# Seven block products for three more batches, in a fused linear attention and mixer kernel

## The chip, the cores and the metric

The kernel runs on one core of one Trainium2 chip. The metric is the device time of one launch in microseconds (us). The kernel before takes 263.8 us, the median of three runs that lie between 263.64 and 263.93 us. One further run was recorded by the profiler, and its span of instructions is 262.1 us. All times "in the trace" are counted from the start of that span.

A core has engines that run their own instruction streams side by side: the tensor engine (PE in the profile, with PEld for its weight loads), the vector engine (DVE), the scalar engine (ACT), the general engine (POOL) and the engine that mostly issues transfers (SP). In the trace each engine runs its instructions in the order in which the program gives them.

## The reference

Eight batches of eight heads, 576 positions and a head width of 64 go through a linear attention, and its output, 576 x 512 for each batch, through a mixer: one two-layer network over the positions, one over the 512 channels with 1536 hidden channels.

```python
phi = lambda x: np.where(x > 0, x, np.exp(x) - 1.0) + 1.0
kv  = einsum('bhsd,bhse->bhde', phi(k), v);  z = phi(k).sum(axis=2)
x   = einsum('bhsd,bhde->bhse', phi(q), kv) / (einsum('bhsd,bhd->bhs', phi(q), z) + 1e-6)
h   = np.maximum(x.T @ w_tok1, 0.0) @ w_tok2       # over the positions, each batch
u   = x + h.T
h2  = np.maximum(u @ w_ch1, 0.0) @ w_ch2           # over the channels: 512 -> 1536 -> 512
out = u + h2
```

The last product, `relu(u @ w_ch1) @ w_ch2`, is the "second channel mixing" that the change is about. In the kernel its left factor is called `cr` (1536 hidden channels on 12 blocks of 128 partitions, 512 positions), and its right factor `wc2`. Of the 576 positions of a batch 512 are handled as four tiles of 128; the 64 that are left over of two neighbouring batches share one more tile, `crt`, called the pair's tail here.

## The kernel before

The program is a hand-made schedule. For each batch `n` from 2 on there is one stretch ("the stage of batch n") in which the tensor engine does the two channel mixings of batch `n`, and everything that batches `n+1` and `n+2` need is dropped in between at numbered places:

```python
    def run(bigs, fill):
        for i, big in enumerate(bigs):
            big()
            for s, fn in fill:          # all that stands at place i, after big number i
                if s == i:
                    fn()
```

The list of large pieces and their fillings, for batches 2 to 7 (before):

```python
    AT = {"kv": 0, "nd00": 2, "nd01": 3, "nd10": 4, "nd11": 5, "nd20": 6, "nd21": 7,
          "mm1": 9, "mm2a": 11, "mm2b": 12, "mm2t": 14, "uta": 11, "utb": 12, "utt": 14}
    for n in range(2, B):
        p, b = divmod(n, 2)
        if b == 0:
            big = m3(n) + (m4s(n) if n + 2 == B else m4(p, [0, 1, 2, 3]))
        else:
            big = m3(n) + m3t + m4(p, [4, 5, 6, 7, 8])
            if n + 1 == B:
                big = m3(n) + m3t + m4s(n) + [ ... mm4_last, in two column pieces ]
        fill = []
        if n + 1 < B:
            fill += [((AT3 if n == 2 else AT)[nm], fn) for nm, fn in steps(n + 1)]
        if n + 2 < B:
            d = 1 if n == 2 else 0
            fill += [(s + d, lambda g=g: phi("q", n + 2, g)) for g, s in ((0, 8), (1, 9))]
            fill += [(12 + d, lambda: qtr_dma(n + 2))]
            ...                                               # loads of batch 5, in stage 2
            fill += [(s + d, lambda g=g: prep_k(n + 2, g)) for g, s in ((0, 14), (1, 16))]
            fill += [(18, lambda: load_all(n + 4, "qkv"))]
        if n + 3 == B:
            fill += [(18 + i, lambda i=i: weight_sums(2 * i, 2)) for i in range(3)]
        if n + 2 >= B:
            fill += [(9, lambda n=n: row_sums(n, 3, 0, KH))]
            fill += [(s, lambda n=n, w=w, k0=k0: row_sums(n, w, k0, 3))
                     for s, k0 in ((10, 0), (12, 3)) for w in (1, 2, 4)]
        run(big, sorted(fill, key=lambda e: e[0]))
```

`m3` is the first channel mixing, 12 pieces of four matmuls of 512 columns; `m3t` is the same for the pair's tail, three pieces. `steps(n+1)` is the attention of the next batch: `kv`, six `nd` pieces (numerators and denominators), `mm1` and `mm2` (the mixing over positions, in two halves a and b, and `mm2t` for the tails of a pair), and the transposes `uta`, `utb`, `utt`, which are transfers. `phi("q", ..)` and `prep_k` prepare the batch after that: an exponential on ACT, then an addition `y` and a minimum (`qp` or `kp`) on DVE.

The second channel mixing is there in two forms. The plain form `m4` does one tile of 128 positions by 12 matmuls of 512 columns and one addition on DVE. The other form, `m4s`, is a scheme with seven block products in place of eight (both factors are cut into 2 x 2 blocks). It is used for batches 6 and 7 before the change:

```python
    def row_sums(n, which, k0, m):      # sums of blocks of cr, on DVE, written into sb[0..3]
        ks = slice(k0, k0 + m)
        a11, a12, a21, a22 = [ablock(n, i, e)[:, ks] for e in range(2) for i in range(2)]
        x_, y_, op = {1: (a21, a22, ALU.add), 2: (sb[0][:, ks], a11, ALU.subtract),
                      3: (a11, a21, ALU.subtract), 4: (a12, sb[1][:, ks], ALU.subtract)}[which]
        nc.vector.tensor_tensor(out=sb[which - 1][:, ks], in0=x_, in1=y_, op=op)

    def product(n, j, i):               # block product i for half j (256 positions)
        lhs, rhs, tile_, first = {
            1: (a_(0, 0), wblock(0, 0), "X", True), 2: (a_(1, 0), wblock(1, 0), "Z", True),
            6: (sb[1][:, :, j], tb[1], "X", False), 5: (sb[0][:, :, j], tb[0], "Y", True),
            7: (sb[2][:, :, j], tb[2], "X", False), 4: (a_(1, 1), tb[3], "X", False),
            3: (sb[3][:, :, j], wblock(1, 1), "Y", False)}[i]
        ...                             # "first" takes a new PSUM bank, the others add onto it
        for k_ in range(KH):            # 6 matmuls of 256 columns
            nc.tensor.matmul(out=ps, lhsT=lhs[:, k_], rhs=rhs[:, k_], start=(first and k_ == 0), ...)
        ...                             # after each of 1, 2, 6, 4, 3 one addition of 128 x 256 on DVE
                                        # from the bank (X, Z or Y) to o_sb; after 7 two (X and Y)
    ORDER = [(1, 0), (1, 1), (2, 0), (6, 0), (2, 1), (6, 1), (5, 0), (7, 0), (5, 1), (7, 1),
             (4, 0), (3, 0), (4, 1), (3, 1)]        # (product, half)
```

So the bank X of a half gets products 1, 6, 7 and 4 added up in it, and DVE reads it after each: product 6 may not start before DVE has read X after product 1, product 7 not before it was read after product 6, and so on. The block sums of the weights, `tb`, are made once by POOL (`weight_sums`, 18 instructions); `tb` and `sb` lie in input buffers whose data are used up.

The inputs of each batch are loaded by SP into `raw[name, n % 2]`, two buffers for each of q, k and v.

## Time and profile before

| what | value |
|---|---|
| time, median of three runs | 263.8 us |
| span of the profiled run | 262.1 us |
| mean granted clock of the tensor engine | 0.992 |
| stage of batch 3 in the trace | from 112.35 to 144.22 us |
| stage of batch 4 | from 144.22 to 171.47 us |
| stage of batch 5 | from 171.47 to 203.34 us |
| stage of batch 6 | from 203.34 to 230.36 us |
| stage of batch 7 and the end | from 230.36 to 262.1 us |

The stages are read from the chain of work that ended last, where each begins with the first piece of `m3`. Where the profile gives a group of instructions, its line has the busy time and the mean duration of one, then the idle time of the engine just before them and what ended that idle time. In a timeline each line is: start, duration, engine, line of the program, operation, output <- inputs with their shapes, the count, and in brackets how long the engine had been idle and what released it. Neighbouring instructions of an engine overlap a little, so the distance between two starts is the better measure of what one costs in a row.

### The profile page before, as it was taken

What the parts mean: (1) busy time and instruction counts of PE and PEld (TensorE: products, weight loads), DVE (VectorE), ACT (ScalarE), POOL (GpSimd) and SP (SyncE); (2) the same over time, 40 slices, a digit from 0 to 9 for tenths busy, and PEclk for the clock granted to TensorE, in tenths of its full rate; (3) what the DMA queues carried; (4) which work ended last, traced back from release to release, by engine and by line L of the source; (5) the groups of instructions that cost most, each with busy time, mean ns of one, the idle gap of its engine ahead of it and who ended that gap; (6) DMA issues with size and microseconds to landing.
All of it is one profiled execution on the core that took longest, in us unless ns stands there. A gap on an engine that the chain in (4) does not pass through costs nothing.

```text
span 262.1 us, 5249 instructions
## 1 busy us (share of the span) xinstructions
PE 249.9 (95%) x2142; PEld 138.4 (53%) x2142; DVE 161.9 (62%) x317; ACT 131.2 (50%) x205; POOL 65.6 (25%) x92
## 2 busy tenths in 40 slices
PE   7799999999999999999999999999999999999990
PEld 3574465646644544455644544455644545756970
DVE  5875859865966376837652575838862486815550
ACT  4755853387580569146670569046670543046100
POOL 9850300110011100110003100179909500060060
PEclk9999999999999999999999999999999999999996
DMA  7999999799049951899999972660083403350033
GB/s 254 254 204 293 351 232 399 243 265 407 9 114 198 393 210 25 179 258 406 409 253 172 373 277 42 149 164 0 16 156 81 123 0 23 80 160 3 0 100 103
DMA packets 49576, 48.35 MB, mean 184 GB/s; under 512 B 30288, under 2 KB 35536, under 8 KB 49552
## 3 DMA queue, kind: packets, MB, share of 16 engines
q1 hardware_dynamic: 41184, 34.35, 43.6%
q0 software_dynamic: 8208, 13.54, 23.3%
q8 instruction: 17, 0.28, 0.5%
q10 hardware_dynamic: 160, 0.13, 0.2%
q14 instruction: 7, 0.06, 0.1%
HBM read 35.85 MB, written 9.44 MB: 173 GB/s over the span
## 4 chain that ended last, share of the span: by engine, by line
PE 79%; DMA 10%; POOL 3%; DVE 2%; issue 1%; ACT 1%; POOLq 0%; DVEq 0%
PE c_ps L480 28%; PE h_ps L506 26%; DMA wc<-in_moe_w_ch_dram 7%; PE a_ps L246 6%; PE c_ps L494 4%; PE h_ps L259 4%; PE nd_ps L208 3%; PE h_ps L605 3%; DMA cr<-in_v_dram 3%; PE kv_ps L167 2%; PE y_ps L605 1%; POOL out_dram L629 1%; DVE o_sb L611 1%; POOL qT L673 1%; DVE ut L284 1%
## 5 line engine op out<-in xcount | busy, mean ns | idle before, releaser
L487 ACT ACTIVATE cr<-c_ps 128x512 bf16<-128x512 f32 x91 | 53.5, 599 | 77.2 <-PE c_ps L480 77.1
L480 PE MATMUL c_ps<-uT,wc 128*128 128x512 bf16 x384 | 91.4, 379 | 0.1
L506 PE MATMUL h_ps<-wc,cr 128*128 128x512 bf16 x288 | 66.0, 379 | 0.4 <-DMA wc<-in_moe_w_ch_dram 0.4
L480 PEld LDWEIGHTS <-wc 128*128 128x128 bf16 x384 | 35.7, 98 | 36.7 <-issue 1.7
L528 POOL DMA_DIRECT2D out_dram<-o_sb x24 | 14.5, 608 | 130.8 <-DVE o_sb L523 130.6
L506 PEld LDWEIGHTS <-cr 128*128 128x128 bf16 x288 | 27.4, 98 | 32.2 <-DMA wc<-in_moe_w_ch_dram 0.9
L220 DVE TENSOR_TENSOR x<-nd_ps,den 128x512 bf16<-128x512 f32 (+1 forms) x42 | 25.3, 602 | 1.5
L523 DVE TENSOR_TENSOR o_sb<-h_ps,u 128x512 f32<-128x512 f32 x24 | 16.4, 689 | 13.2 <-PE h_ps L506 13.0
L124 ACT ACTIVATE e<-q_raw 128x1152 bf16<-128x1152 f32 x16 | 18.5, 1160 | 5.6 <-DMA q_raw<-in_q_dram 5.4
L138 DVE TENSOR_TENSOR qp<-e,y 128x1152 bf16<-128x1152 bf16 x16 | 12.3, 770 | 12.3 <-ACT e L124 11.8
L124 ACT ACTIVATE e<-k_raw 128x1152 bf16<-128x1152 f32 x16 | 18.7, 1169 | 2.4 <-DMA k_raw<-in_k_dram 2.4
L217 DVE TENSOR_SCALAR den<-nd_ps 128x8 f32<-128x8 f32 (+1 forms) x42 | 6.9, 163 | 19.9 <-PE nd_ps L208 19.2
L271 DVE TENSOR_TENSOR u<-h_ps,x 128x1024 bf16<-128x1024 f32 x12 | 14.7, 1222 | 6.2 <-PE h_ps L259 6.2
L629 POOL DMA_DIRECT2D out_dram<-o_sb x16 | 8.3, 527 | 40.4 <-DVE o_sb L611 40.4
L138 DVE TENSOR_TENSOR kp<-e,y 128x1152 bf16<-128x1152 bf16 x16 | 12.1, 757 | 8.0 <-ACT e L124 7.4
L208 PEld LDWEIGHTS <-qT 128*128 128x128 bf16 x140 | 11.4, 98 | 9.3 <-issue 0.2
L208 PE MATMUL nd_ps<-kvbd,qT 128*128 128x130 bf16 x140 | 15.1, 223 | 0.0
L246 PE MATMUL a_ps<-x,w 128*128 128x512 bf16 x56 | 14.4, 379 | 0.0
L130 DVE TENSOR_SCALAR y<-q_raw 128x1152 bf16<-128x1152 f32 x16 | 13.6, 849 | 0.9 <-DMA q_raw<-in_q_dram 0.9
L149 ACT CAST vs<-v_raw 128x1152 bf16<-128x1152 f32 x12 | 13.9, 1160 | 0.0
L130 DVE TENSOR_SCALAR y<-k_raw 128x1152 bf16<-128x1152 f32 x16 | 12.0, 753 | 1.4 <-DMA k_raw<-in_k_dram 1.3
L259 PE MATMUL h_ps<-ar,w2p 128*128 128x512 bf16 x48 | 12.3, 379 | 0.0
(120 smaller groups left out, 282.9 us busy)
## 6 DMA issues: line engine op xcount, KB each, us to landing
k_raw<-in_k_dram SPq DMA_DIRECT2D x16, 576.0 KB, 9.8
q_raw<-in_q_dram SPq DMA_DIRECT2D x16, 576.0 KB, 7.1
v_raw<-in_v_dram SPq DMA_DIRECT2D x14, 576.0 KB, 11.1
out_dram<-o_sb POOLq DMA_DIRECT2D x24, 256.0 KB, 5.0
wc<-in_moe_w_ch_dram POOLq DMA_DIRECT2D x8, 384.0 KB, 9.3
out_dram<-o_sb POOLq DMA_DIRECT2D x22, 128.0 KB, 3.4
cr<-in_v_dram POOLq DMA_DIRECT2D x2, 288.0 KB, 6.9
w<-in_moe_w_tok_dram POOLq DMA_DIRECT2D x1, 288.0 KB, 7.2
```

The costliest lines, as they stand in the source:

```text
L124: nc.scalar.activation(out=e, in_=f, func=AF.Exp)
L130: nc.vector.tensor_scalar(out=y, in0=f, scalar1=1.0, scalar2=1.0, op0=ALU.add, op1=ALU.max)
L138: nc.vector.tensor_tensor(out=dst.transpose([0, 2, 1, 3]), in0=e.rearrange("p (i t d) -> p i t d", i=nj, t=T), in1=y.rearrange("p (i t d) ...
L208: nc.tensor.matmul(out=o[:, a], lhsT=qT[b][:, t0:t0 + 128], rhs=kvbd[b][:, c, a], start=True, stop=True)
L220: nc.vector.tensor_tensor(out=x[b][:, rs[0]:rs[0] + m, HG * D * g:HG * D * (g + 1)].rearrange("p r (h d) -> p r h d", h=HG), in0=v_[:, :, ...
L246: nc.tensor.matmul(out=ps[:, mt], lhsT=w1t[:, b, ms] if r == R else w1[:, r, ms], rhs=x[b][:, r, :], start=(r == 0), stop=(r == R))
L259: nc.tensor.matmul(out=ps[:, i], lhsT=w2v(kt, r, b), rhs=ar[b][:, kt, :], start=(kt == 0), stop=(kt == NT - 1 and not add))
L271: nc.vector.tensor_tensor(out=u[b][:, rs[0]:rs[0] + m], in0=ps[:, 0:m], in1=x[b][:, rs[0]:rs[0] + m], op=ALU.add)
L480: nc.tensor.matmul(out=ps, lhsT=wc1[:, kj, 128 * mc:128 * mc + 128], rhs=uT[b][:, :, kj], start=(kj == 0), stop=(kj == NDM - 1))
L487: nc.scalar.activation(out=cr[b][:, mc, :], in_=ps, func=AF.Relu)
L506: nc.tensor.matmul(out=ps, lhsT=crt[:, kc, :] if t == 8 else cr[b][:, kc, 128 * r:128 * r + 128], rhs=wc2[:, kc, :], start=(kc == 0), stop ...
L523: nc.vector.tensor_tensor(out=o, in0=ps, in1=u[b][:, r, :], op=ALU.add)
```

## The change

The seven block products are used for batches 3 to 7 in place of 6 and 7. The sums of the weights have to be there earlier: they go into stage 2, and lie with `sb` in the second of the input buffers. From batch 4 on therefore all loads go to the first buffer. The tails of pairs stay in the plain form. Some places of fillings move with it: `prep_k` comes later, and `mm2t` of the stages of even batches comes last in its stage. In the last stage the products of one half come before those of the other, and the last tail (`m4(3, [8])`) comes ahead of the last two products; its output leaves through SP and ACT in place of POOL. The aim is less work for the tensor engine: 14 x 6 matmuls of 256 columns in place of 4 x 12 of 512 for each batch.

```diff
+    def rb(n):
+        return n % 2 if n < 4 else 0
-        return after(nc.sync.dma_start(out=raw[nm, n % 2][:, js], in_=src_[:, js]), gate)
+        return after(nc.sync.dma_start(out=raw[nm, rb(n)][:, js], in_=src_[:, js]), gate)
 # ... (the readers of raw likewise; mm4_last is gone)
+    FIRST = 3
+    tb = [bf("k", 1, i).rearrange("p (k c) -> p k c", k=KH) for i in range(3)] + [
+        bf("q", 1, 0).rearrange("p (k c) -> p k c", k=KH)]
+    tf = raw["q", 1].rearrange("p j f -> p (j f)")[:, 768:2304].rearrange("p (k c) -> p k c", k=KH)
+    sb = [(bf("v", 1, i) if i < 3 else bf("q", 1, 1)).rearrange("p (k j s) -> p k j s", k=KH, j=2)
           for i in range(4)]
 # ... in product:
-        if i in (4, 3):
-            d, r = (1 if i == 4 else 0), 2 * j + (1 if i == 4 else 0)
+        queues = [nc.sync, nc.scalar] if n + 1 == B else [nc.gpsimd] * 2
+        if n + 1 == B and j == 1 and i in (2, 4, 3):
+            d, cs = {2: (0, HC[0]), 4: (1, ALL), 3: (0, HC[1])}[i]
             for e in range(2):
-                nc.gpsimd.dma_start(out=outv[n, :, 2 * r + e], in_=o[half[e], d])
+                queues[e].dma_start(out=outv[n, :, 2 * (2 * j + d) + e, cs], in_=o[half[e], d, cs])
+        elif i == 3:
+            for e in range(2):
+                queues[e].dma_start(out=outv[n, :, 4 * j + e:4 * j + e + 3:2], in_=o[half[e]])
+    LAST = [(1, 0), (2, 0), (6, 0), (5, 0), (7, 0), (1, 1), (4, 0), (3, 0),
+            (2, 1), (6, 1), (5, 1), (7, 1), None, (4, 1), (3, 1)]      # None: the tail, m4(3, [8])
 # ... in the loop over the stages:
         if b == 0:
-            big = m3(n) + (m4s(n) if n + 2 == B else m4(p, [0, 1, 2, 3]))
+            big = m3(n) + (m4s(n) if n >= FIRST else m4(p, [0, 1, 2, 3]))
         else:
-            big = m3(n) + m3t + m4(p, [4, 5, 6, 7, 8])
-            if n + 1 == B:
-                big = m3(n) + m3t + m4s(n) + [
-                    lambda: mm4_last(slice(0, DM - 128)), lambda: mm4_last(slice(DM - 128, DM))]
+            big = m3(n) + m3t + (m4(p, [4, 5, 6, 7, 8]) if n < FIRST else
+                                 m4s(n) + m4(p, [8]) if n + 1 < B else m4s(n, LAST))
         if n + 1 < B:
-            fill += [((AT3 if n == 2 else AT)[nm], fn) for nm, fn in steps(n + 1)]
+            at_ = dict(AT3 if n == 2 else AT)
+            if n >= FIRST:
+                at_.update(mm2t=25, utt=25)
+            fill += [(at_[nm], fn) for nm, fn in steps(n + 1)]
         if n + 2 < B:
 # ...
-            if n == 2:
-                fill += [(16, lambda: load_all(5, "qkv"))]
-            fill += [(s + d, lambda g=g: prep_k(n + 2, g)) for g, s in ((0, 14), (1, 16))]
-            fill += [(18, lambda: load_all(n + 4, "qkv"))]
-        if n + 3 == B:
-            fill += [(18 + i, lambda i=i: weight_sums(2 * i, 2)) for i in range(3)]
-        if n + 2 >= B:
+            k_ = ((14, 16) if n < FIRST else (18, 20) if b == 0 else (14, 21))
+            fill += [(s + d, lambda g=g: prep_k(n + 2, g)) for g, s in enumerate(k_)]
+            fill += [(k_[1] + 2, lambda: load_all(n + 3, "qkv"))]
+        if n + 1 == FIRST:
+            fill += [(4 * i, lambda i=i: weight_sums(2 * i, 2)) for i in range(3)]
+        if n >= FIRST:
             fill += [(9, lambda n=n: row_sums(n, 3, 0, KH))]
             # ... the other row_sums as before, places 10 and 12
```

More of the change, by code (lines that the diff above doesn't have):

```diff
@@ L121, in phi_exp @@
     def phi_exp(nm, n, j0, nj):
-        f = raw[nm, n % 2][:, j0:j0 + nj].rearrange("p j f -> p (j f)")
+        f = raw[nm, rb(n)][:, j0:j0 + nj].rearrange("p j f -> p (j f)")
         e = work.tile([128, 2 * TD], BF16, name="e", tag="e", bufs=4)[:, :nj * TD]
@@ L127, in phi_add @@
     def phi_add(nm, n, j0, nj):
-        f = raw[nm, n % 2][:, j0:j0 + nj].rearrange("p j f -> p (j f)")
+        f = raw[nm, rb(n)][:, j0:j0 + nj].rearrange("p j f -> p (j f)")
         y = work.tile([128, 2 * TD], BF16, name="y", tag="y")[:, :nj * TD]
@@ L149, in vcast @@
         copy(out=vs[:, js, :, 0:D],
-             in_=raw["v", n % 2][:, js].rearrange("p j (t d) -> p j t d", t=T))
+             in_=raw["v", rb(n)][:, js].rearrange("p j (t d) -> p j t d", t=T))
     def bank():
@@ L535, in mm4_end @@
                 put.dma_start(out=outv[2 * p + b, :, 2 * R], in_=o[half[b]])
-    def mm4_last(cs):
-        p = B // 2 - 1
-        m = cs.stop - cs.start
-        ps = ps_big.tile([128, 512], FP32, name="h2_ps", tag="big")[:, 0:m]
-        for kc in range(NCH):
-            nc.tensor.matmul(out=ps, lhsT=crt[:, kc, :],
-                             rhs=wc2[:, kc, cs], start=(kc == 0), stop=(kc == NCH - 1))
-        o = outp.tile([128, 2, DM], FP32, name="o_sb", tag="o_sb")[:, 0, 0:m]
-        nc.vector.tensor_tensor(out=o, in0=ps, in1=ut[p % 2][:, cs], op=ALU.add)
-        for b in range(2):
-            (nc.scalar if b else nc.sync).dma_start(out=outv[2 * p + b, :, 2 * R, cs],
-                                                    in_=o[half[b]])
     KH = NCH // 2
@@ L557, in bf @@
         return t[:, 1536 * i:1536 * (i + 1)]
-    tb = [bf("k", 0, i).rearrange("p (k c) -> p k c", k=KH) for i in range(3)] + [
-        bf("q", 0, 0).rearrange("p (k c) -> p k c", k=KH)]
-    tf = raw["q", 0].rearrange("p j f -> p (j f)")[:, 768:2304].rearrange("p (k c) -> p k c", k=KH)
-    sb = [(bf("v", 0, i) if i < 3 else bf("v", 1, 0)).rearrange("p (k j s) -> p k j s", k=KH, j=2)
+    FIRST = 3
[3 more added lines that the diff above has]
+    sb = [(bf("v", 1, i) if i < 3 else bf("q", 1, 1)).rearrange("p (k j s) -> p k j s", k=KH, j=2)
           for i in range(4)]
@@ L625, in product, with m4s @@
             add(0, 1, ps, o[:, 0, HC[1]])
-        if i in (4, 3):
-            d, r = (1 if i == 4 else 0), 2 * j + (1 if i == 4 else 0)
+        queues = [nc.sync, nc.scalar] if n + 1 == B else [nc.gpsimd] * 2
+        if n + 1 == B and j == 1 and i in (2, 4, 3):
+            d, cs = {2: (0, HC[0]), 4: (1, ALL), 3: (0, HC[1])}[i]
             for e in range(2):
-                nc.gpsimd.dma_start(out=outv[n, :, 2 * r + e], in_=o[half[e], d])
+                queues[e].dma_start(out=outv[n, :, 2 * (2 * j + d) + e, cs], in_=o[half[e], d, cs])
+        elif i == 3:
+            for e in range(2):
+                queues[e].dma_start(out=outv[n, :, 4 * j + e:4 * j + e + 3:2], in_=o[half[e]])
     ORDER = [(1, 0), (1, 1), (2, 0), (6, 0), (2, 1), (6, 1), (5, 0), (7, 0), (5, 1), (7, 1),
              (4, 0), (3, 0), (4, 1), (3, 1)]
-    def m4s(n):
-        return [lambda i=i, j=j: product(n, j, i) for i, j in ORDER]
+    LAST = [(1, 0), (2, 0), (6, 0), (5, 0), (7, 0), (1, 1), (4, 0), (3, 0),
+            (2, 1), (6, 1), (5, 1), (7, 1), None, (4, 1), (3, 1)]
+    def m4s(n, order=ORDER):
+        out_ = []
+        for e in order:
+            out_ += [lambda e=e: product(n, e[1], e[0])] if e else m4(n // 2, [8])
+        return out_
     def prep_k(n, g, copy=nc.scalar.copy):
```

## The prediction

> **What bounds the kernel now.** First the busy times and the 40 slices of the page.

> ```profile
> PE 249.9 (95%) x2142; PEld 138.4 (53%) x2142; DVE 161.9 (62%) x317; ACT 131.2 (50%) x205; POOL 65.6 (25%) x92
> ...
> PE   7799999999999999999999999999999999999990
> ...
> DVE  5875859865966376837652575838862486815550
> ```

> From the third slice on the tensor engine is never under nine tenths, so time is PE work plus PE waits. DVE has room on average; its slices between 25% and 90% say that the average hides something. Next the chain of waits, for stage 4 (start 144.22):

> ```profile
> 158.73 0.86 PE h_ps L259 x4
> 159.59 0.86 PE h_ps L506 x4
> 160.45 0.86 PE h_ps L259 x4
> 161.32 1.73 PE h_ps L506 x8
> 163.04 0.55 PE h_ps L280 x4
> 163.60 7.88 PE h_ps L506 x36
> 171.47 0.86 PE c_ps L480 x4
> ```

> L259 is `mm2a` and `mm2b`, L506 the plain second mixing, L280 `mm2t`. There is no gap: four matmuls of 512 columns are 0.863 us. Then DVE's own timeline in the same stage:

> ```profile
> 155.70 0.76 DVE L138 TENSOR_TENSOR qp<-e,y 128x1152 bf16<-128x1152 bf16 x1 [1.04 <-ACT e L124]
> 156.37 0.75 DVE L130 TENSOR_SCALAR y<-q_raw 128x1152 bf16<-128x1152 f32 x1
> 159.21 0.76 DVE L138 TENSOR_TENSOR qp<-e,y 128x1152 bf16<-128x1152 bf16 x1 [2.08 <-ACT e L124]
> 159.88 1.22 DVE L271 TENSOR_TENSOR u<-h_ps,x 128x1024 bf16<-128x1024 f32 x1
> 161.35 1.22 DVE L271 TENSOR_TENSOR u<-h_ps,x 128x1024 bf16<-128x1024 f32 x1 [0.26 <-PE h_ps L259]
> ```

> DVE sits idle for ACT's exponential, and is free for other work only at 159.88, 15.66 us into the stage. That is harmless in the plain form. Last, how the product form runs in stage 6, from the timeline:

> ```profile
> 213.03 1.42 DVE L587 TENSOR_TENSOR v_raw<-cr 128x1536 bf16<-128x1536 bf16 x2
> 214.48 0.56 DVE L587 TENSOR_TENSOR v_raw<-v_raw,cr 128x768 bf16<-128x768 bf16 x1
> ...
> 222.59 0.56 DVE L587 TENSOR_TENSOR v_raw<-cr,v_raw 128x768 bf16<-128x768 bf16 x1
> ...
> 223.06 0.42 DVE L611 TENSOR_TENSOR o_sb<-h_ps,u 128x256 f32<-128x256 f32 x1
> ...
> 223.73 1.38 DVE L284 TENSOR_TENSOR ut<-h_ps,x 64x512 bf16<-64x512 f32 x2
> ...
> 225.62 0.82 PE L605 MATMUL h_ps<-k_raw,v_raw 128*128 128x256 bf16 x6 [0.54 <-DVE o_sb L611]
> ```

> L587 are the row sums, L611 the additions after products. The first row sums begin 9.7 us into this stage, because stage 6 has no `phi` any more. Even so PE waits for a DVE addition at 225.62.

> [...] 0.863/4 = 0.216 us, and in stage 7 the chain has 36 of 256 columns in 3.93 us, 0.109 each, 0.656 for a product. [...] 768 bf16 take 0.56 us, 1024 from PSUM 1.22. [...] in this trace POOL's 1.16 us subtraction takes 1.67 and DVE's `y` 1.13 to 1.72 instead of 0.75 where they meet (181 to 187 us). The weight sums now meet stage 2.

> **The change part by part.**

> PE work. Per batch 48 x 0.216 = 10.36 us become 84 x 0.1093 = 9.18 us: 1.18 us less, for batches 3, 4 and 5, thus 3.5 us if PE never waits.

> DVE work per changed stage. Added: one row sum of 1536 (0.87 in a row), six of 768 (0.59 each), 14 additions of 256 (0.34 each where independent): 9.2 us. Removed: four additions of 512, 0.6 each: 2.4 us. Stage 4 goes from about 17.7 busy to over 24 us, in a stage that should last 26. What counts is where it lies.

> Stage 3 (odd; also 5), in us from the stage's start. The built order of DVE is: second `qp`, row sum 3, three row sums, both `u`, three row sums, `y`, `kp`, and only then the addition after product (1,0). DVE is free for it at 15.66 as before. Row sums: 15.66 + 0.87 + 2 x 0.59 + 0.47 (the last of a chain, 222.59 to 223.06) = 18.18. Two `u`, 1.15 apart: 20.47. Three row sums: 22.12. `y` to `kp` is 0.86 and `kp` 0.68 (from 165.10, 165.96, 166.64): 23.66. The addition ends at 23.66 + 0.42 = 24.08. PE reaches the products at 131.27 - 112.35 = 18.92, does (1,0), (1,1), (2,0) until 20.89, and (6,0) has to wait for that addition: about 24.14, a hole of 3.25 us. After it 11 products remain, 11 x 0.656 = 7.2, to 31.36. I followed DVE through them: each later addition comes at least 0.2 us before PE needs it. The tail, 12 x 0.216 = 2.59, ends at 33.95 where the stage took 31.87 before: +2.08 us. Stage 5 is the same list: +2.08.

> Stage 4. PE ends `mm2a` at 15.37 and (1,0) at 16.03, `mm2b` at 16.89, (2,0) at 18.20. DVE: row sums until 18.18, `u` a, addition (1,0) at 19.33, `u` b at 19.70, row sums from 20.84; the second half of sb[1], which (6,0) multiplies, is written at 21.99. So the second half of (6,0) starts near 22.05 and ends near 22.38 where it could have ended at 18.86: 3.5 us lost. Then two `prep_k` stand in DVE's queue ahead of the additions after (7,0) and (7,1), 1.54 us each: the read of X after (7,1) ends near 28.5, PE would want it at 27.6, and loses another 0.9. (4,1) and (3,1) to 29.88, `mm2t` 0.55: 30.43 against 27.25: +3.18 us.

> Stage 6. `mm2t` goes from a place where PE waited anyway (221.47) to the end, and with its two 0.69 us additions out of the way the 0.7 us wait for product (7,0) is gone: -0.7 + 0.55 = -0.15 us.

> Stage 7. The same PE work: 14 x 0.656 + 2.59 = 11.77 us from 243.40 on, as before. But SP now has four transfers in a row at the end, 0.6 each (two took 1.19), behind additions that end at 254.6 to 255.6, and so issues its last near 256.45 instead of 255.75: +0.5 us, my choice for this.

> Loads and weight sums. SP's queue has the loads of batch 6 behind `uta`, `utb` and the `qT` transposes of stage 3; they can be issued from about 26 us into the stage, the k loads after the last `y` at 27.4. A k load lands in 9.8 us and a q load in 7.1, so by about stage 4's 5th us, and q is wanted at its 10th, k at its 19th. Stage 4 to 5 is alike. I count nothing. The weight sums on POOL, 18 x 1.16 = 21 us, lie in stage 2 (84.93 to 112.35), where the plain form leaves DVE room: nothing.

> Sum: 2 x 2.08 + 3.18 - 0.15 + 0.5 = 7.7 us. I take 7.4, a little less, since each distance in a row was taken from a busy stretch: 263.8 + 7.4 = 271.2 us.

> **The rivals.**

> Rival A, PE stays the bound. The product stretch would flow as in stage 7, where the trace has it almost without waits: 3.5 us less, 260.3 us. For it: DVE's 62%. Against it: stage 7 has no `phi`, no `u` and no `prep_k` in DVE's queue, and stage 6, which lacks only `phi` and `prep_k`, gained 27.25 - 27.02 = 0.23 us of the 1.18 on paper.

> Rival B, the loads. With one buffer, a load can't start until the last reader is done; if PE's stages are stretched and the readers late, the exponential of q in the next stage would wait, and ACT's relus behind it, and PE would stop when its four `c_ps` banks are full. For it: load time of up to 11 us. Against it: the five us of slack above. It would add 2 to 4 us in stages 4 and 5: 274 us.

> Rival C, POOL and DVE block each other in stage 2 so much that `u` and its transposes for stage 3 come late. Before, the last `u` starts at 103.09 and its transfer was issued by 105.57, seven us ahead of stage 3. Four `y` and `qp` delayed by 1 us each don't use that up: under 0.5 us.

> **Range and chances.** The two holes in stages 3 and 5 rest on a plain queue order and measured durations, so I am sure of their existence and within some 0.7 us of each size; stage 4 is less sure, since two waits follow each other. If PE finds work elsewhere or the additions come 1 us sooner in each stage, it is 268.2; with some of rival B 273.5. The boundary of 2% is 269.1. Slower by over 2%: 0.80. Within 2%: 0.17. Faster by over 2%: 0.03, as even rival A gives only 1.3%.

> **What would show it.** In the timeline of stages 3 and 5: an idle time of PE of about 3.2 us ahead of the first product that reads `sb`, released by DVE's addition to `o_sb`; in stage 4 one of about 3.5 us in the middle or ahead of the same product, released by a row sum, and a smaller one near the end; the stages should last about 34, 30.4, 34 and 26.9 us. `kp` of stage 3 should stand between the last row sum and the first addition. PE's busy time in matmuls should fall while the span grows. I am wrong if stage 3 lasts 30.7 us with no hole (rival A), if ACT shows waits for q or k transfers of over 1 us in stages 4 or 5 (rival B), or if stage 2 grows (rival C).

## The result and the profile after

The changed kernel takes 274.28 us (median of four runs, 274.13 to 274.91) against 263.83 us: 1.040 times the time before, with a 95% interval of 1.038 to 1.042. The change makes the kernel slower by 10.5 us. The prediction was 271.2 us with a range to 273.5: the direction is right, the size 3.1 us too small and out of its range.

First the same lines of the page as before, with the row of the granted clock.

```profile
PE 252.3 (93%) x2224; PEld 150.4 (55%) x2238; DVE 182.8 (67%) x367; ACT 131.0 (48%) x205; POOL 60.9 (22%) x80
...
PE   7899999999999999999599995999959999899992
...
DVE  6874668856774778595964659868596375862552
...
PEclk9999999999999999999979999799997999999997
```

The row of the clock in the page of the kernel before is:

```profile
PEclk9999999999999999999999999999999999999996
```

The tensor engine now has three slices of five tenths, which it had nowhere in the middle before. The row of the clock has a 7 right after each of them, and that is new too. By stages, from the chain of waits (the first piece of `m3` of each) and the stretches between them:

| stage | before, us | predicted | after | after minus before |
|---|---|---|---|---|
| 3 | 31.87 | 33.95 | 35.90 | +4.03 |
| 4 | 27.25 | 30.43 | 31.64 | +4.39 |
| 5 | 31.87 | 33.95 | 35.83 | +3.96 |
| 6 | 27.02 | 26.87 | 26.88 | -0.14 |
| 7 and the end | 31.74 | 32.24 | 30.02 | -1.72 |

The sum of the last column is 10.5 us. Stage 6 is as predicted; three stages lost more than predicted, and the end gained where a loss was predicted. Now the timeline of VectorE in stage 3 (from 112.23 us on), to be held against the list of the prediction:

```profile
127.23 0.76 DVE L141 TENSOR_TENSOR qp<-e,y 128x1152 bf16<-128x1152 bf16 x1 [2.08 <-ACT e L127]
127.90 1.42 DVE L577 TENSOR_TENSOR v_raw<-cr 128x1536 bf16<-128x1536 bf16 x2
...
130.50 2.35 DVE L274 TENSOR_TENSOR u<-h_ps,x 128x1024 bf16<-128x1024 f32 x2
...
134.01 0.56 DVE L577 TENSOR_TENSOR q_raw<-cr,v_raw 128x768 bf16<-128x768 bf16 x1
...
134.48 0.75 DVE L133 TENSOR_SCALAR y<-k_raw 128x1152 bf16<-128x1152 f32 x1
...
135.34 0.76 DVE L141 TENSOR_TENSOR kp<-e,y 128x1152 bf16<-128x1152 bf16 x1
136.01 0.75 DVE L601 TENSOR_TENSOR o_sb<-h_ps,u 128x256 f32<-128x256 f32 x2
```

VectorE is free for row sums at 15.67 us of the stage (predicted 15.66), works without a stop, and starts the first addition at 23.78 (predicted 23.66). That is the queue that was predicted, `kp` between the last row sum and the first addition included. And the timeline of the tensor engine there:

```profile
130.99 2.13 PE L595 MATMUL h_ps<-wc,cr 128*128 128x256 bf16 x18
136.49 1.43 PE L595 MATMUL h_ps<-k_raw,v_raw 128*128 128x256 bf16 x6 [3.37 <-DVE o_sb L601]
137.72 1.49 PE L595 MATMUL h_ps<-wc,cr 128*128 128x256 bf16 x6
139.00 1.30 PE L595 MATMUL h_ps<-k_raw,v_raw 128*128 128x256 bf16 x6
140.13 0.82 PE L595 MATMUL y_ps<-k_raw,v_raw 128*128 128x256 bf16 x6
140.79 0.82 PE L595 MATMUL h_ps<-k_raw,v_raw 128*128 128x256 bf16 x6
```

Three products, then a hole of 3.37 us that VectorE's addition ends (predicted 3.25). What was not predicted stands in the start times after it: from 136.49 to 137.72, to 139.00 and to 140.13, a product takes 1.23, 1.28 and 1.13 us; from 140.13 on it is 0.66 again. The windows of the trace give the clock granted in each microsecond (columns: from:to, length, busy time and count of PE, PEld, DVE, ACT, POOL, then the granted clock, the share of the transfer engines and GB/s):

```profile
132.00:136.40 4.40, 1.12 (x11) 0.75 (x8) 4.16 (x8) 3.99 (x4) 0.00 (x0) 1.00 0.72 129
136.40:137.40 1.00, 0.91 (x5) 0.66 (x6) 0.70 (x3) 0.00 (x0) 0.00 (x0) 0.58 0.70 176
137.40:138.40 1.00, 1.00 (x7) 0.67 (x6) 0.42 (x1) 0.00 (x0) 0.00 (x0) 0.50 0.75 182
138.40:139.40 1.00, 1.00 (x6) 0.69 (x5) 0.16 (x1) 0.00 (x0) 0.00 (x0) 0.50 0.69 172
139.40:140.40 1.00, 1.00 (x9) 0.78 (x7) 0.33 (x2) 0.00 (x0) 0.00 (x0) 0.71 0.89 132
140.40:141.40 1.00, 1.00 (x12) 0.90 (x10) 1.00 (x2) 0.00 (x0) 0.00 (x0) 1.00 0.98 371
```

```profile
167.92 0.49 PE L595 MATMUL h_ps<-k_raw,v_raw 128*128 128x256 bf16 x3 [1.59 <-DVE o_sb L601]
170.12 0.50 PE L595 MATMUL h_ps<-k_raw,v_raw 128*128 128x256 bf16 x3 [1.71 <-DVE v_raw L577]
```

The theory to test: the holes come from the order of VectorE's queue, the rest of the loss from the clock that the holes drop. Rivals: the products after the hole are slow for another reason (they read sums just written); VectorE has too much work whatever its order; the single load buffers or the early sums of the weights cost something of their own.

### The profile page after: what moved, and what is told of

Read it like the earlier page. It is cut to its first block, busy times and chain, and to the rows that moved or that the text cites. A ratio compares the mean times of both kernels' runs of the same rounds, so it can differ in the third digit from the quotient of the medians.

```text
span 272.5 us, 5473 instructions
## 1 busy us (share of the span) xinstructions
PE 252.3 (93%) x2224; PEld 150.4 (55%) x2238; DVE 182.8 (67%) x367; ACT 131.0 (48%) x205; POOL 60.9 (22%) x80
## 4 chain that ended last, share of the span: by engine, by line
PE 69%; DVE 11%; DMA 7%; ACT 5%; issue 3%; POOL 3%; SPq 0%; DVEq 0%; POOLq 0%; ACTq 0%
PE c_ps L483 25%; PE h_ps L509 14%; PE h_ps L595 10%; PE a_ps L249 5%; PE y_ps L595 4%; DMA k_raw<-in_k_dram 4%; DVE v_raw L577 4%; DMA wc<-in_moe_w_ch_dram 4%; PE nd_ps L211 3%; DVE u L274 3%; ACT e L127 2%; PE c_ps L497 2%; PE kv_ps L170 2%; PE h_ps L262 2%; DVE o_sb L601 1%
## 5 line engine op out<-in xcount | busy, mean ns | idle before, releaser
L623 POOL DMA_DIRECT2D out_dram<-o_sb x16 | 9.6, 606 | 114.3 <-DVE o_sb L601 114.0
L509 PE MATMUL h_ps<-wc,cr 128*128 128x512 bf16 x139 | 34.0, 379 | 0.4
L595 PE MATMUL h_ps<-k_raw,v_raw 128*128 128x256 bf16 x120 | 19.2, 300 | 10.6 <-DVE o_sb L601 8.2
L595 PEld LDWEIGHTS <-v_raw 128*128 128x128 bf16 x180 | 19.2, 108 | 15.8 <-issue 5.2
L601 DVE TENSOR_TENSOR o_sb<-h_ps,u 128x256 f32<-128x256 f32 x40 | 16.6, 420 | 9.2 <-PE h_ps L595 9.1
L509 PEld LDWEIGHTS <-cr 128*128 128x128 bf16 x144 | 13.5, 98 | 15.1 <-issue 0.7
L595 PEld LDWEIGHTS <-cr 128*128 128x128 bf16 x180 | 18.0, 101 | 4.0 <-issue 0.4
L531 POOL DMA_DIRECT2D out_dram<-o_sb x12 | 7.4, 619 | 47.6 <-DVE o_sb L526 47.6
L595 PE MATMUL h_ps<-wc,cr 128*128 128x256 bf16 x120 | 16.8, 290 | 0.0
L141 DVE TENSOR_TENSOR kp<-e,y 128x1152 bf16<-128x1152 bf16 x16 | 12.9, 805 | 3.9 <-ACT e L127 2.9
L577 DVE TENSOR_TENSOR v_raw<-cr 128x768 bf16<-128x768 bf16 (+1 forms) x15 | 9.9, 685 | 7.1 <-ACT cr L490 7.1
## 6 DMA issues: line engine op xcount, KB each, us to landing
v_raw<-in_v_dram SPq DMA_DIRECT2D x14, 576.0 KB, 10.5
```

The lines of the kernel that those rows point to most:

```text
L141: nc.vector.tensor_tensor(out=dst.transpose([0, 2, 1, 3]), in0=e.rearrange("p (i t d) -> p i t d", i=nj, t=T), in1=y.rearrange("p (i t d) ...
L509: nc.tensor.matmul(out=ps, lhsT=crt[:, kc, :] if t == 8 else cr[b][:, kc, 128 * r:128 * r + 128], rhs=wc2[:, kc, :], start=(kc == 0), stop ...
L601: add = lambda e, c, x_, y_: nc.vector.tensor_tensor(out=o[:, e, HC[c]], in0=x_, in1=y_, op=ALU.add)
```

## The experiments

Each kernel is compared with the kernel before on the same chip. All edits are to the changed kernel, except where said.

**1. Filling the holes with useless matmuls.** The queue of VectorE is as in the changed kernel; the tensor engine works on a bank that is overwritten afterwards.

```diff
+    def dummy(m):
+        if "z1" not in live:
+            live["z1"] = ps_big.tile([128, 512], FP32, name="h2_ps", tag="big")   # bank Z of half 1
+        for _ in range(m):
+            nc.tensor.matmul(out=live["z1"], lhsT=identity, rhs=wc2[:, 0, :], start=True, stop=True)
+        if FIRST <= n < 6:
+            fill += [(17, lambda: dummy(14))] if n % 2 else [(14, lambda: dummy(7))]
 # and dummy(7) in stage 4 between the third and fourth matmul of product (6, 0)
```

> Changed kernel with useless matmuls of 512 columns put where the tensor engine stood idle: 14 (3.0 us) ahead of product 6 in stages 3 and 5, 7 ahead of it and 7 inside it in stage 4. The queue of VectorE is untouched, so the waits stay. Theory (the idle time drops the tensor engine's clock to half, and the products after it pay for it: 1.95 + 1.2 + 1.9 us): clock 1.00 through these stages, stages of about 34.0, 30.4 and 33.9 us, time about 269.3. Rival (the products after the hole are slow because they read sums that were just written, or because VectorE holds them up): nothing changes, 274.3, and with each us of filler that overhangs a little more.

Measured: 269.89 us (269.64 to 270.14), 4.4 less than the changed kernel; stages of 34.23, 30.52 and 34.17 us. The timeline of the tensor engine in stage 3 of this kernel, and the windows of stages 3 to 5:

```profile
133.28 3.19 PE L585 MATMUL h_ps<-wc,identity 128*128 128x512 bf16 x14
136.82 0.83 PE L607 MATMUL h_ps<-k_raw,v_raw 128*128 128x256 bf16 x6 [0.35 <-DVE o_sb L613]
137.49 0.82 PE L607 MATMUL h_ps<-wc,cr 128*128 128x256 bf16 x6
```

```profile
112.56:146.79 34.23, 33.88 (x318) 21.58 (x316) 23.73 (x51) 16.76 (x25) 3.59 (x6) 1.00 0.76 239
146.79:177.31 30.52, 29.48 (x261) 17.72 (x260) 23.29 (x50) 14.96 (x22) 1.73 (x4) 1.00 0.53 154
177.31:211.48 34.17, 33.97 (x317) 21.69 (x318) 24.37 (x51) 16.76 (x25) 4.14 (x7) 1.00 0.53 149
```

The same product that took 1.23 us starts the next one 0.67 us later, and it is still VectorE's addition that it waits for. The rival falls: nothing about the operands has changed. Work that computes nothing makes the kernel faster by 4.4 us; that is about the price of the clock in the changed kernel (1.67 + 1.12 + 1.66 us by stages). What is left, 34.2, 30.5 and 34.2 us, is the prediction without the clock to within 0.3 us.

**2. A shorter hole.** One preparation of k in the odd stages leaves VectorE's queue ahead of the first addition.

```diff
-            k_ = (... else (18, 20) if b == 0 else (14, 21))
+            k_ = (... else (18, 20) if b == 0 else (20, 22))
```

> Changed kernel with the first preparation of k in the odd stages at place 20 in place of 14, so that 1.54 us of VectorE work leave the queue ahead of the first addition: the hole of stages 3 and 5 shrinks from 3.3 to about 1.8 us. Theory (clock): each of the two stages gains 1.54 us of waiting and 1.9 us of half clock, 6.9 together, time about 267.5, clock 1.00 in both stages, stage 4 as it was. Rival (only the wait counts): 3.1 us less, 271.2.

Measured: 269.72 us (268.89 to 270.52). The holes are 1.84 and 1.69 us, the clock is 1.00 in stages 3 to 5, and the two odd stages take 33.63 and 33.58 us, about 2.3 less each. Expected were 3.4 less: with both preparations at 20 and 22 they stand one behind the other ahead of the additions after product 7, and the tensor engine loses 0.94 us ahead of product (4,1) in each odd stage (1.53 + 1.67 - 0.94 = 2.3). The edit made a new wait, so the expected time was missed, but in the stages the share of the clock is there again. In this run stage 4, whose waits are those of the changed kernel, kept its clock too (30.51 us). So a drop isn't certain for a given wait; experiment 4 comes back to that.

**3. The hole made longer step by step.** The kernel of experiment 2, with one row sum repeated (same values): once in stage 3, twice in stage 5.

```diff
+            fill += [(12, lambda n=n: row_sums(n, 4, 3, 3)) for _ in range({3: 1, 5: 2}.get(n, 0))]
```

> The kernel with the late preparation of k, where VectorE repeats one row sum of 768 once in stage 3 and twice in stage 5 (the same values are written again), so the holes are about 2.4 and 3.0 us. Theory: there is a length of idle time between 1.8 and 3.3 us from which the clock drops; if it lies above 3.0, no stage but 4 shows a drop and the stages cost 0.6 and 1.2 us more than without the repeats; if the drop comes already at 2.4 or 3.0, that stage costs 1.9 us more on top. Rival (only the wait counts): 0.6 and 1.2 us more.

Measured: 273.37 us (one run). The hole of 2.43 us in stage 3 cost its 0.6 us and no more (34.22 us, clock 1.00). The hole of 2.88 us in stage 5 dropped the clock (0.95 over the stage, 36.36 us: 2.78 more than in experiment 2, where two repeats are 1.2). Stage 4 dropped here, with the same 1.59 and 1.70 us of waiting that left the clock alone in experiment 2.

**4. A hole with work in its middle.** Three useless matmuls in the holes of stages 3 and 5, held back by a row sum that they read.

```diff
+        for _ in range(3):
+            nc.tensor.matmul(out=live["z1"], lhsT=sb[3][:, 3, 0], rhs=wc2[:, 0, :], start=True, stop=True)
```

> Changed kernel with three useless matmuls of 512 columns (0.65 us) in the middle of the hole of stages 3 and 5: they read a row sum, so that they run about 1.3 us after the hole begins and end about 1.3 us ahead of its end. VectorE's queue is untouched. If the clock drops after one stretch of idle time of about 2.5 us or more, no drop in stages 3 and 5 and about 271.0. If the share of idle time in some longer stretch counts, drops as before, in some executions or in all, 272 to 274.5, and stage 4 (1.6 and 1.7 us of waiting with 0.3 us of work between) shows which.

Measured: 272.05 us, with single runs from 270.24 to 274.32, a spread that no other kernel here has. The timeline of the tensor engine of the profiled run, stage 3 and then stage 5:

```profile
134.77 0.82 PE L585 MATMUL h_ps<-wc,q_raw 128*128 128x512 bf16 x2 [1.50 <-DVE q_raw L577]
136.64 1.44 PE L605 MATMUL h_ps<-k_raw,v_raw 128*128 128x256 bf16 x6 [1.04 <-DVE o_sb L611]
...
202.21 0.82 PE L585 MATMUL h_ps<-wc,q_raw 128*128 128x512 bf16 x2 [1.36 <-DVE q_raw L577]
204.08 0.81 PE L605 MATMUL h_ps<-k_raw,v_raw 128*128 128x256 bf16 x6 [1.04 <-DVE o_sb L611]
```

Nearly the same two waits, and one product at half speed in stage 3 (1.44 us of duration), at full speed in stage 5 (0.81). So the length of one gap alone does not decide: the clock dropped here after gaps of 1.50 and 1.04 us, and in experiment 3 it did not after one of 2.43.

Next the work just ahead of a drop. In the changed kernel the trace's record of the clock is at 0.50 from 136.56, 170.69 and 204.83 us on, for 3.41 us each time, and in the 3.41 us ahead of these times the tensor engine worked for 0.07, 1.06 and 0.85 us. Here are, for stage 3 and then stage 5 of this run, a stretch of about that length that holds waits and the one after it (columns as above):

```profile
133.17:136.58 3.41, 0.87 (x3) 0.31 (x4) 3.17 (x7) 2.97 (x3) 0.00 (x0) 1.00 0.86 163
136.58:140.00 3.42, 3.36 (x16) 2.31 (x16) 1.51 (x5) 0.00 (x0) 0.00 (x0) 0.50 0.79 172
201.44:204.85 3.41, 1.54 (x10) 1.00 (x12) 3.10 (x7) 2.28 (x3) 0.00 (x0) 1.00 0.85 177
204.85:208.26 3.41, 3.41 (x34) 3.06 (x32) 2.77 (x6) 0.00 (x0) 0.00 (x0) 1.00 0.43 103
```

In stage 3 the tensor engine worked for 0.87 us of the first stretch, and has half the clock in the second. In stage 5 it worked for 1.54 us of the first, and the clock stays. But the hole of 2.43 us in experiment 3, from 132.99 to 135.42 us, leaves only 0.98 us of work in the 3.41 us ahead of its end, less than the 1.06 us above, and the products after it start 0.66 us apart, at the full rate. So the work just ahead does not decide alone either; what does was not shown.

The four runs of this experiment spread with the clock: its mean is 0.995 in the run of 270.24 us, 0.992 in that of 271.43, 0.985 in that of 272.67 and 0.981 in that of 274.32.

**5. Another order for VectorE.** The work of every engine stays the same. The row sums go into the two stretches in which VectorE waits for the exponential of q, the last three of them ahead of the second `u` or of the additions, and the preparations of k go to places where products are not waiting.

```diff
+            phi_(phi_exp, 0); phi_(phi_add, 0)
+            add(8, row_sums, n, 3, 0, KH)                 # in the first wait for the exponential
+            phi_(phi_end, 0); phi_(phi_exp, 1); phi_(phi_add, 1)
+            for wh in (1, 2, 4):
+                add(9, row_sums, n, wh, 0, 3)             # in the second
+            phi_(phi_end, 1)
+            # last three row sums at 12; mm2b's u at 12 (odd) or, split from its matmuls at 14, at 15 (even)
-            k_ = (... (18, 20) if b == 0 else (14, 21))
+            k_ = (17, 26) if b else (21, 23)
```

> Changed kernel with VectorE's queue in another order in stages 3 to 6: row sums inside the two stretches in which it waits for the exponential of q, the last three row sums ahead of the second u in odd stages and ahead of the additions in even ones, both preparations of k later. Same work on every engine. Theory (holes come from the order of VectorE's queue, and the rest of the loss from the clock that the holes drop): no hole over 0.7 us, clock 1.00, stages of about 30.8, 26.4, 30.8 and 26.5 us, time about 259.5 to 261. Rival (VectorE has too much work in these stages, whatever its order): the holes move to other products, time over 265.

Measured: 258.93 us (258.2 to 259.92), 0.981 of the time before (0.978 to 0.984), and once more beside the second attempt of experiment 6, on another chip, with this expectation:

> The first reordered kernel once more, beside the other on the same chip: 258 to 260, no hole over 0.7 us, clock 1.00 from stage 3 to 6.

It was 259.23 us, 0.983 (0.981 to 0.985). The windows of stages 3, 4 and 5 in the trace of the first of these:

```profile
112.80:143.42 30.62, 30.62 (x304) 20.30 (x302) 23.79 (x51) 16.77 (x25) 3.28 (x6) 1.00 0.73 238
143.42:170.07 26.65, 26.10 (x248) 16.50 (x247) 21.79 (x47) 14.97 (x22) 1.77 (x4) 1.00 0.55 159
170.07:202.20 32.13, 31.01 (x303) 20.34 (x304) 25.70 (x54) 16.77 (x25) 4.17 (x8) 1.00 0.79 201
```

VectorE is as busy in stage 3 as in the changed kernel (23.8 us), the tensor engine has no idle time at all, and the stage takes 30.6 us where the sum of the tensor engine's work was 30.7. So in stage 3 the loss was the order, not the amount. From stage 4 on the rival has a part: VectorE is busy for 15.8 of the 17 us from 155 to 172 us, and waits of 0.55 us (`mm2t`, in stage 4) and 0.61 us (`kv`, in stage 5) for it stay. Stage 5 waits another 0.52 us for the transpose of the tail, and takes 32.13 us, more than the 31.87 of the plain form (30.8 expected). Stages 3 to 5 take 89.4 us in sum, against 91.0 before the change: 1.6 of the 3.5 us that the products save on paper. The rest of what this kernel gains is stage 6 (25.96 against 27.02 us) and the end (29.94 against 31.74).

**6. Two attempts on what is left.** From experiment 5 on: first both the second preparation of k and the loads moved to the end of stage 4, then the loads alone.

```diff
-                k_ = (17, 26) if b else (21, 23)
+                k_ = (17, 26) if b else (21, 25)           # first attempt only
-                fill.append((k_[1] + 1, lambda: load_all(n + 3, "qkv")))
+                # behind the transpose of the tail in even stages, in both attempts
```

> The kernel with the other order of VectorE's queue, with two places moved in stages 4: the second preparation of k after the additions of the tail, and the loads of batch 7 after the transpose of the tail. In its trace before this edit kv of stage 5 waits 0.61 us for an addition that stood behind that preparation, mm2t 0.55 us for another, and the tail of stage 5 0.52 us for the transpose that stood behind the loads. Theory: these 1.7 us go, time about 257.3. Rival (the waits move on, since VectorE is full in stage 4): 258.9, as without the edit.

Measured: 260.39 us, 0.987 (0.985 to 0.990), no gain. I had overlooked that the next stage begins with `kv`, which reads that `kp`. The timeline of the tensor engine has it:

```profile
172.65 0.48 PE L170 MATMUL kv_ps<-vs,kp 64*64 64x65 bf16 x36 [1.75 <-DVE kp L141]
```

> The first reordered kernel (second preparation of k ahead of the last additions) with one place moved: in stage 4 the loads of batch 7 stand behind the transpose of the tail in SP's queue. Theory: the 0.52 us wait of stage 5's tail for that transpose goes, 0.5 us less than the first reordered kernel on the same chip; the waits of mm2t and kv for VectorE (0.55 and 0.61 us) stay, as VectorE is full in stage 4. Rival (the loads, now later, are waited for in stage 5): as much or more than it.

Measured: 258.94 us (258.81 to 259.14), against 259.23 for experiment 5 on the same chip, 0.981 (0.980 to 0.983). The wait for the transpose is gone in its trace, but it is gone in the second trace of experiment 5 too, without the edit; stage 5 takes 31.46 us in both, and the difference of 0.3 us is less than the spread of the other's runs. So the edit is not shown to do anything. The wait of `kv` is there with 0.60 us. VectorE has little room from 155 us on, and these two attempts did not get round it; others were not tried.

**7. The seven products left out of batches 3 to 5.** The plain form there; single load buffers, early weight sums, the tail of stage 6 and the last stage as in the changed kernel.

```diff
-            big = m3(n) + (m4s(n) if n >= FIRST else m4(p, [0, 1, 2, 3]))
+            big = m3(n) + (m4s(n) if n >= 6 else m4(p, [0, 1, 2, 3]))
 # likewise for odd n, the row sums and the late mm2t
```

> Changed kernel, with the plain form of the second mixing in batches 3 to 5; single load buffers, early sums of the weights, late preparation of k, the places of the tails in stage 6 and the last stage as in the changed kernel. Theory (only the seven products in stages 3 to 5 cost time; buffers and sums are hidden; stage 6 gains 0.15 and the end 1.7 us): 262.0. Rival (single buffers or the early sums cost 1 us or more in stages 2 to 5): 263 to 266, with waits for q or k transfers on the scalar engine.

Measured: 262.19 us, 0.994 (0.992 to 0.996). The windows of its stages 2 to 7:

```profile
84.80:112.13 27.33, 27.33 (x212) 13.00 (x211) 20.67 (x34) 15.08 (x22) 25.53 (x22) 1.00 0.65 195
112.13:144.00 31.87, 31.87 (x267) 16.76 (x266) 17.29 (x34) 16.77 (x25) 3.60 (x6) 1.00 0.77 249
144.00:171.26 27.26, 27.26 (x211) 12.96 (x210) 17.69 (x34) 14.97 (x22) 2.29 (x4) 1.00 0.54 158
171.26:203.13 31.87, 31.87 (x267) 16.77 (x266) 17.12 (x33) 16.76 (x25) 3.60 (x6) 1.00 0.69 187
203.13:230.00 26.87, 26.13 (x248) 16.37 (x246) 18.01 (x42) 8.89 (x16) 2.17 (x4) 1.00 0.21 46
230.00:260.00 30.00, 24.98 (x192) 16.61 (x192) 12.18 (x24) 8.96 (x15) 1.31 (x3) 1.00 0.35 84
```

Stages 3 to 5 last what they lasted before the change, to 0.01 us, with one load buffer each. In stage 2 POOL is busy with the weight sums for most of the time (25.5 us), and VectorE's busy time rises to 20.7 us, but the tensor engine has no gap. Rivals B and C of the prediction are nothing here. Nor are they in the changed kernel, whose stages are longer: in its stages 4 and 5 the scalar engine waits for the tensor engine alone, never for a load, and its stage 2 takes 27.35 us (27.42 before). The gain is the end, 30.00 against 31.74 us.

**8. The end: which queue the last output takes.** First the kernel before, with only the queues of batch 7's products changed; then the changed kernel, with POOL's queue put back.

```diff
-                nc.gpsimd.dma_start(out=outv[n, :, 2 * r + e], in_=o[half[e], d])
+                (nc.gpsimd if n + 1 < B else (nc.sync, nc.scalar)[e]).dma_start(
+                    out=outv[n, :, 2 * r + e], in_=o[half[e], d])
```

> Kernel before, with one edit: the output of batch 7's products leaves through SP and ACT in place of POOL. Theory (the end of the changed kernel is short, 4.6 us from the last VectorE instruction to the end of the span against 6.6, because POOL has no transfers at the end): about 2 us less, 261.8, and the last 6.6 us shrink to about 4.6. Rival (the order of the last stage makes it): no change, 263.8.

Measured: 261.31 us, 0.990 (0.988 to 0.992), 2.6 us less than before.

```diff
-        queues = [nc.sync, nc.scalar] if n + 1 == B else [nc.gpsimd] * 2
+        queues = [nc.gpsimd] * 2
```

> Changed kernel, with one edit: the last batch's products send their output through POOL again, in the same pieces. Theory (POOL's transfers at the end cost the 2 us): 276.3. Rival (the order of the last stage makes it): 274.3.

Measured: 276.39 us (275.40 to 277.32), 2.1 us more than the changed kernel. In its trace stage 4 kept its clock (30.51 us), so the whole mixes two effects. The last stage alone, from its first piece of `m3` to the end of the span, is clearer:

| last stage and the end, us | POOL's queue | SP's and ACT's queues |
|---|---|---|
| order and pieces before | 31.74 | 29.07 |
| order and pieces of the change | 32.66 | 30.02 |

The queue is worth 2.6 to 2.7 us in either order. The new order and pieces cost 0.9 us with either queue, so the end gained by the queue alone. The view of SP's own waits at the end, before the change:

```profile
SPq L895 <- DMA out_dram<-o_sb: 3.0, 2, 2.8
SPq L895 <- PEq L895: 2.0, 2, 1.5
```

and in the kernel before with the other queues:

```profile
SPq L896 <- DMA out_dram<-o_sb: 1.6, 3, 0.7
SPq L896 <- PEq L896: 0.7, 2, 0.5
```

(columns: us in total, times, longest). The last addition ends 6.6 us ahead of the end of the span before the change (255.52 and 262.1), and 3.9 with the other queues (255.89 and 259.8): the waits for the last transfers and between the engines at the end are 2.7 us shorter in sum. Which of POOL's steps takes that time was not tried.

## Why the prediction was right and wrong

- **The bound and the queue** (PE bound; VectorE free for row sums only at 15.66 us): right. Starts in stage 3 agree to 0.12 us. One sign failed: PE's busy time was to fall, and rose from 249.9 to 252.3 us, because the products at half rate count as busy for longer: in stage 3 it is 32.42 us, against 30.62 in the first trace of experiment 5, which has none.
- **The holes**: right in place, releaser and size: 3.25 predicted, 3.37 and 3.23 measured in stages 3 and 5; in stage 4 two waits ahead of product (6,0) and inside it, the first for an addition and the second for the row sum, 1.59 and 1.71 us with 0.3 us of work between (3.5 predicted), and a late one ahead of (4,1), 0.22 us where 0.9 was predicted, because the slowed products had given VectorE time (0.77 in experiment 1, where they are not slowed). Without the clock (experiment 1) the stages take 34.23, 30.52 and 34.17 where 33.95, 30.43 and 33.95 were predicted.
- **The step that failed** is the one after each hole: "After it 11 products remain, 11 x 0.656 = 7.2". The products were taken at the full rate, though the engine had just been idle for over three microseconds. Three of them ran at half clock. The term that was missing measured 1.67 + 1.12 + 1.66 = 4.45 us in the changed kernel (experiment 1 taken away). The sizes fit the record of the clock: 3.41 us at half clock lose 1.71 us of work, and in stage 4 some 0.55 us came back through the shorter wait ahead of (4,1). The profile before could not show it: the tensor engine's longest wait between 20 and 250 us is 0.54 us there.
- **Stage 6**, -0.15 us: right, -0.14.
- **Stage 7**, +0.5 us: wrong in sign, -1.72. The prediction charged for more transfers in a row on SP. The new order and pieces do cost 0.9 us, but with either queue, so that its reason is not shown. What was missing is the worth of the queue, 2.6 to 2.7 us less (experiment 8): the prediction looked at the time at which transfers are issued, and not at the 6.6 us from the last addition to the end of the span. Its row of slices ends in a 0, which the sentence below it, "never under nine tenths", passed over.
- **Loads and weight sums**, nothing: right (experiment 7). **Rival A**, 260.3 us if VectorE's queue flows: it did not in the changed kernel, but experiment 5, which only reorders that queue and has the new end, reaches 258.9, though 1.8 us of it are the end, which rival A did not count.

In sum: the predicted 7.4 us, plus 4.45 for the clock, minus 2.2 for the end, plus the 0.3 that were taken off, plus 0.6 for holes a little longer than on paper (0.28 + 0.09 + 0.22, experiment 1 against the prediction), is the measured 10.5.

## What to carry to other kernels

Before an engine that isn't the bottleneck is given more work, write down its queue in order and look for the instruction that the bottleneck waits for: an average of 67% says nothing of an addition that stands behind 5.5 us of other work (130.50 to 136.01 in stage 3 of the changed kernel). A hole of about three microseconds in the tensor engine's stream cost up to 1.7 us more here, since the products after it ran at half clock for a while (3.41 us in the changed kernel). Holes of 2.88 to 3.37 us did so each of five times, those of 1.69 to 2.43 us did not, two waits close together did in four cases of seven, and the runs of one kernel differed (270.24 to 274.32 us in experiment 4). The row of the granted clock and the start times of equal pieces show it, and busy time hides it. And the way from the last computed value to the end of the span is a stage of its own: here the choice of the queue for the last outputs was worth 2.6 to 2.7 us, more than the products save on paper in two odd stages (31.87 to 30.7 us each).

## What was not expected of the hardware

- In stages 3 to 5 of the changed kernel, of experiments 2 to 4 and of the second kernel of experiment 8 the tensor engine's clock fell to half after nine holes: five single ones of 2.88 to 3.37 us, one of two waits of 1.50 and 1.04 us, and three of two waits of 1.59 and 1.70 or 1.71 us with three matmuls between. It stayed after six: single ones of 1.69, 1.84 and 2.43 us, one of two waits of 1.36 and 1.04 us, and two of two waits of 1.59 and 1.70 or 1.58 and 1.71 us. Why the same pair dropped the clock in some kernels only was not shown.
- The first product after a hole twice still ran at the full rate, and the three after it at about half: in stage 5 of the changed kernel it starts at 203.98 us and the next ones at 204.63, 205.72, 207.00 and 208.26, and the record of the clock falls at 204.83; in stage 3 of the second kernel of experiment 8 the starts are 136.48, 137.14, 138.33, 139.61 and 140.78 us.
- Useless work can be worth its time: 42 matmuls that compute nothing made the changed kernel 4.4 us faster. Reordering beat that by 11 us.
